# Eight inverse stages taken in pairs, and their banks copied into the product planes

## The chip, the cores and the metric

The kernel runs on one core of one Trainium2 chip. The time is the device time of one execution in microseconds. One execution was also recorded by the hardware profiler; its trace is what the sections below read. PE is the matrix engine, PEld its weight loads, DVE the vector engine, ACT the scalar engine, POOL GpSimd, SP the engine that issues most transfers. PSUM is the memory that PE writes to, eight banks of 128x512 fp32; SBUF is the memory that the other operands lie in.

## The reference

Two branches of one input `x` (2048 x 512), mixed by a gate:

```python
x = A_q
g = _sigmoid((x * gate_w).sum(-1, keepdims=True))
a = _A_ref(x, A_k, A_v, A_shift_k, A_ssm_k, A_ssm_D)
b = _B_ref(x, B_w1, B_w2)          # relu(x @ w1) @ w2, inner width 1792
return g * a + (1 - g) * b
```

The first branch is a long causal convolution over the 2048 positions, for each of 512 channels:

```python
kv = k_shift * v                   # k_shift: 4 taps along the positions
kv_f = rfft(kv padded to 4096)
kf_f = rfft(ssm_k padded to 4096)
y = irfft(kv_f * kf_f)[:2048]
y = y + kv * ssm_D
return q * y
```

## The kernel before

**The MLP branch.** The positions are cut into four chunks of 512, the inner width into 14 tiles. fp32 operands are split into a high and a low part (`xh`, `xl` of x, `hh`, `hl` of the hidden layer, the weights likewise), and each product is three matmuls of 128x512: `mlp1` (L376 to L378) writes a bank `m`; ACT takes `hh` from it (L389), DVE `hl` (L392); `mlp2` (L406 to L408) reads both. The xl parts are made by `split` (L302, `xl_l<-raw,xh_h`), a subtraction that the planner gives to DVE or to POOL. The y sums (L429) take a bank of `mlp2` each. On PE these matmuls are one long stream, and everything else interrupts it.

**The convolution branch.** A transform in two stages. Stage 1 (`s1h`, `s1x`, L459) is over before the place of the change; its result lies in DRAM (`sa`). What follows goes in eight groups g = 0 to 7. For each group a *chain* of PE work, one uninterrupted piece, stands in `conv_mid`: two rounds `f_h` and two rounds `f_x` (L575), 16 small matmuls each on a quarter of the array, into two banks a round. ACT and DVE take `f_h` over into `ha` (L604, L609). Then DVE multiplies (L617): the first product writes `p`, a tile of four planes of 128x512, and four more write `ha`, `qa`, `qb` and `ha` again (called a to e in the code). POOL adds these to `p` in eight sums (L623).

**The inverse.** `inverse(g)` (L642 to L652) reads `p` and the constants `cc` of group g and writes four banks `iv`, with 32 matmuls: one matmul to each bank in turn, eight times. `put_iv` (L654 to L665) empties these banks, DVE the banks 0 and 2 (L664), ACT the banks 1 and 3 (L662), into tiles `bv`, and each tile is stored to DRAM (`sb`, L659). When all is stored, `conv_end` reads it back (`br`) and ends the transform (`cy`, L727).

**Which inverse stands where.** The inverse of group g - 2 (`BEHIND`) stands at the start of the chain of group g; a ninth chain holds the last two inverses, 6 and 7, in a row.

**What sets the order.** The class `Plan` holds all operations with their needs and makes the order of each engine before the program is built, from durations written in the kernel. `room` (L266) says how many buffers of each kind there are: `cv` 8 (PSUM banks), `p` 2 (`PB`), `cc` 3, `bv` 4, `ha` 2, `qa` and `qb` 1. An operation takes and gives back rooms. A PE operation with `pair` waits for a favourable place in the stream, at most the time that `LONG` has for its kind. On each engine the instructions run in the order made; a wait holds up all that stands behind on that engine. The numbers of the banks are dealt out in turn.

Of the kernel before, what the change touches and what calls it, by code (L numbers as in the profile page):

```python
# [13 lines left out]
S, D, DFF = 2048, 512, 1792  # L14
# [3 lines left out]
NJ = 32  # L18
# [216 lines left out]
def act_time(n, psum=False):  # L235
    return n * 0.000833 + (0.05 if psum else 0.093)


def dve_time(n):
    return n * 0.001042 + 0.12  # L240
# [3 lines left out]
TILES = 0.865  # L244
SWITCH = 0.19
ROW = P * D * 4


def build(tc, wf, xp, qn, kn, vn, hn, dn, sh, gw, w1, w2, cs1, ccf, cci, cib, out):
    nc = tc.nc  # L250
# [11 lines left out]
    sb = dram.tile([P, 32, D], F32, name="sb")  # L262

    yd = dram.tile([P, 4, D], F32, name="yd")

    room = {"raw": RAW, "x": 4, "cv": 8, "hh": HB, "o": OB, "in": IN, "cc": BEHIND + 1, "cf": 2, "qa": 1, "qb": 1, "acc": ACC, "tmp": TMP, "ev": EV, "r": RB,  # L266
            "yr": 2, "ha": HAB, "p": PB, "bv": BVB, "br": BRB, "t": TB, "j": 1, "q": QB, "w1": WB, "w2": WB}
    plan = Plan(room)
    add = plan.add
    T = {}  # L270
    cpool = [None, None]

    def tile_of(key, tag, w=D, dt=F32, bufs=None, rows=P, p=None):
        nm = tag + "_" + "_".join(map(str, key[1:] if len(key) > 1 else key))
        T[key] = (p or cpool[0]).tile([rows, w], dt, tag=tag, bufs=bufs or room.get(tag, 1), name=nm)
        return T[key]
# [255 lines left out]


    sbstores = []
    ys, rtags = {}, {}

    def conv_load(g, gate):
        rank = 500.0 + 4 * g
        k = lambda *nm: (*nm, g)
        rtag = lambda t, u: "yr" if (4 * g + 2 * "hx".index(t) + u) % 6 > 3 else "r"  # L540

        def load(t, u):
            tag = rtag(t, u)

            def ld():
                tile_of(k("r", t, u), tag, 2 * D, p=mp if tag == "yr" else None)
                j = 4 * g + 2 * u
                nc.sync.dma_start(rows(T[k("r", t, u)]), sa["hx".index(t), :, j:j + 2])

            return add("SP", ISSUE, rank + 0.1 * u + (0 if t == "h" else 1), ld, [gate], [tag], dma=2 * ROW, fifo=[tag])  # L550

        cc = [add("SP", ISSUE, rank - 0.5, lambda: nc.sync.dma_start(tile_of(k("cf"), "cf", 2 * P), ccf[:, g]), [gate], ["cf"], dma=ROW // 2, fifo=["cf"]),
              add("SP", ISSUE, rank + 1.5, lambda: nc.sync.dma_start(tile_of(k("cc"), "cc", P), cci[:, g]), [gate], ["cc"], dma=ROW // 4, fifo=["cc"])]
        for t in "hx":
            rtags[g, t] = [rtag(t, u) for u in range(2)]
        return [load("h", u) for u in range(2)], [load("x", u) for u in range(2)], cc

    def conv_mid(g, gate):

        rank = (1, 500.0 + 4 * g)  # L560
        k = lambda *nm: (*nm, g)
        tt = nc.vector.tensor_tensor
        chain = []

        def link(dur, fn, deps, take, give=(), pair=0):
            o = add("PE", dur, (0, rank), fn, (deps if not chain else [chain[-1]]), take, give, tiles=True, pair=pair)
            chain.append(o)
            return o

        def rounds(t, o):  # L570
            ps = [bank(k("f", t, o, b)) for b in range(2)]
            for j in range(4):
                for b in range(2):
                    at = slice(64 * b, 64 * b + 64)
                    mm(ps[b][32 * j:32 * j + 32, :], T[k("cf")][at, 64 * j + 32 * o:64 * j + 32 * o + 32],  # L575
                       T[k("r", t, j // 2)][at, (j % 2) * D:(j % 2 + 1) * D], start=True, stop=True)

        old = g - BEHIND
        last = ys.get(old, [])
        if g < NJ // 4:  # L580
            h, x, cc = conv_load(g, gate)
            deps = h + x + cc + last
        else:
            deps = last
        olds = [old] if g < NJ // 4 else range(old, NJ // 4)
        deps = deps + [y for o in olds[1:] for y in ys[o]]
        for o in olds:
            if o >= 0:
                put_iv(o, link(2 * TILES, lambda o=o: inverse(o), deps, ["cv"] * 4, ["p", "cc"], 3 if g == NJ // 4 else 4 if o == olds[0] else 0))
        if g >= NJ // 4:  # L590
            plan.chain(chain)
            return
        planes = lambda z, u, n=2: T[k(z)][:, u * D:(u + n) * D].rearrange("p (r d) -> p r d", d=D)
        ha, fh = [], []
        for o in range(2):
            f = link(TILES, lambda o=o: rounds("h", o), deps, ["cv"] * 2 + ([] if o else ["ha"]), rtags[g, "h"] if o else ())
            fh.append(f)

        plane = lambda i: T[k("ha")][:, i * D:(i + 1) * D]

        def lower(o):
            if not o:
                tile_of(k("ha"), "ha", 4 * D)
            nc.scalar.copy(plane(o), T[k("f", "h", o, 0)])  # L604

        for o in range(2):
            ha.append(add("ACT", act_time(D, True), (0, rank), lambda o=o: lower(o), [fh[o]] + ha[:1], (), ["cv"]))
        for o in (1, 0):
            ha.append(add("DVE", dve_time(D), (0, rank), lambda o=o: tt(plane(2 + o), T[k("f", "h", o, 1)], plane(1 - o), op=OP.add if o else OP.subtract),  # L609
                          [fh[1], ha[1 - o]], (), ["cv"]))  # L610
        fx = [link(TILES, lambda o=o: rounds("x", o), deps, ["cv"] * 2 + ([] if o else ["p"]), [*rtags[g, "x"], "cf"] if o else ()) for o in range(2)]

        def mul(o, b, dst, u, src, n, deps, take=(), give=(), w=None):
            def go():
                if w:
                    tile_of(k(dst), w[0], w[1] * D)
                tt(planes(dst, u, n), T[k("f", "x", o, b)][:, None, :].to_broadcast([P, n, D]), planes("ha", src, n), op=OP.mult)  # L617

            return add("DVE", dve_time(n * D), rank, go, [fx[o], *deps], take, give)

        def sums(dst, src, u, n, deps, sign=1, give=()):
            def go():
                nc.gpsimd.tensor_tensor(planes("p", dst, n), planes("p", dst, n), planes(src, u, n), op=OP.add if sign > 0 else OP.subtract)  # L623

            return add("POOL", 0.11 + n * 1.14, rank, go, deps, (), give)

        a = mul(0, 0, "p", 0, 0, 4, ha, give=["cv"], w=("p", 4))
        b = mul(1, 0, "ha", 2, 2, 2, [a])
        c = mul(1, 0, "qa", 0, 0, 2, [b], ["qa"], ["cv"], ("qa", 2))
        d = mul(0, 1, "qb", 0, 0, 2, [c], ["qb"], ["cv"], ("qb", 2))  # L630
        e = mul(1, 1, "ha", 0, 0, 2, [d], give=["cv"])
        z = sums(3, "ha", 2, 1, [b])
        z = sums(2, "ha", 3, 1, [z], -1)
        z = sums(1, "qa", 0, 1, [z, c])
        z = sums(0, "qa", 1, 1, [z], -1, ["qa"])
        z = sums(2, "qb", 0, 1, [z, d])
        z = sums(3, "qb", 1, 1, [z], 1, ["qb"])
        z = sums(3, "ha", 0, 1, [z, e])
        z = sums(2, "ha", 1, 1, [z], -1, ["ha"])
        ys[g] = [z]  # L640
        plan.chain(chain)

    def inverse(g):
        k = lambda *nm: (*nm, g)
        ps = [bank(k("iv", j)) for j in range(4)]
        for o in range(2):
            for b in range(2):
                for j in range(4):
                    at = slice(32 * j, 32 * j + 32)
                    c = 64 * o  # L650
                    z = (2 * b + o) * D
                    mm(ps[j][64 * b:64 * b + 64, :], T[k("cc")][at, c:c + 64], T[k("p")][at, z:z + D], start=o == 0, stop=o == 1)  # L652

    def put_iv(g, iv):  # L654
        rank = (1, 500.0 + 4 * g)
        k = lambda *nm: (*nm, g)
        for j in range(4):
            def put(j=j):
                nc.sync.dma_start(sb[:, 4 * g + j], T[k("bv", j)])  # L659

            if j % 2:
                bv = add("ACT", act_time(D, True), rank, lambda j=j: nc.scalar.copy(tile_of(k("bv", j), "bv"), T[k("iv", j)]), [iv], ["bv"], ["cv"])  # L662
            else:
                bv = add("DVE", dve_time(D), (0, rank), lambda j=j: nc.vector.tensor_copy(tile_of(k("bv", j), "bv"), T[k("iv", j)]), [iv], ["bv"], ["cv"])  # L664
            sbstores.append(add("SP", ISSUE, (-5000, rank), put, [bv], (), ["bv"], dma=ROW))  # L665


    def finish(n, key, rank, deps, give):
        parts = 2 if n == LAST else 1
# [142 lines left out]

DEBUG = None
SHARE = 0.0
LONG = 50.0, 50.0, 12.0, 0.0
KEEP = 0
SLOW = dict(raw=1.0)
PATIENCE = 0.5
BEHIND = 2
G = 4  # L820
WARM = 9
DMA_AHEAD = 2.0
# [6 lines left out]
ISSUE = 0.47  # L829
IV_FIRST = True  # L830
RAW = 4
WB = 7
HB = 7
TB = 5
OB = 2
# [3 lines left out]
TMP = 1  # L839
RB = 4  # L840
HAB = 2
PB = 2
BVB = 4
BRB = 4
QB = 8
X0 = -31.0
# [44 lines left out]
```

## Time and profile before

| | us |
|---|---|
| median of 3 runs | 385.6 (385.55 to 386.24) |
| the profiled execution | 385.97 |
| its span in the trace | 384.2 |
| PE busy | 379.8 |
| DVE busy | 266.7 |
| ACT busy | 128.8 |
| POOL busy | 91.5 |

The page of the profile gives busy time, the span in 40 slices with the granted clock, the queues, the chain of work that ended last, and the costliest groups. The time outside the span is 1.77 us. A row of the timeline has the start in us from the span's start, the length, the engine, the line, the operation with out<-in, the shape, the number of instructions in the row, and in brackets how long the engine stood idle before it and what ended that. The ends of matmuls are modelled, so the length of a PE stage is read from the start of one stage to the start of the next.

The chains stand in the trace at 183.4 (g = 0), 193.4, 202.7, 219.3, 232.5, 245.7, 258.9, 272.1 (g = 7) and 295.5 (the ninth).

### The profile page before, as it was taken

Reading aid. Unit: us, or ns where it says so; the run is one execution under the profiler, and the core shown is the slowest. Engines: PE = TensorE matmul, PEld = TensorE weight load, DVE = VectorE, ACT = ScalarE, POOL = GpSimd, SP = SyncE. Lnnn points to the kernel's source line nnn. Section 1 sums busy time; section 2 is a strip of 40 time slices with the busy share of each in tenths; the row PEclk is TensorE's granted clock in tenths of the full one; section 3 lists DMA queues with packets and bytes.
Section 4 is the critical chain, followed back from the end, with each engine's and each line's share of the span. In section 5 each row is a group of like instructions: output and inputs, shape, how many; then the busy total and the mean of one; then the engine's idle time right before and its main releaser. Section 6 shows DMA issues by size and latency. Waiting matters only on the chain.

```text
span 384.2 us, 6567 instructions
## 1 busy us (share of the span) xinstructions
PE 379.8 (99%) x2505; PEld 273.8 (71%) x2505; DVE 266.7 (69%) x356; ACT 128.8 (34%) x242; POOL 91.5 (24%) x77
## 2 busy tenths in 40 slices
PE   9999999999999999999999999999999999999996
PEld 5888788668877788788655765565587788688684
DVE  4698999797989028114799687897872347687691
ACT  5643524573147525533224022313400333012100
POOL 0000000000000000000199968866995001000000
PEclk9999999999999999999999999999999999999999
DMA  7997893898648763589867876686460798399331
GB/s 274 368 317 255 298 351 113 293 333 323 208 121 330 295 234 109 185 296 275 285 203 238 307 265 227 241 308 232 139 204 3 241 342 320 120 325 357 117 124 56
DMA packets 43474, 92.51 MB, mean 241 GB/s; under 512 B 4625, under 2 KB 7201, under 8 KB 43442
## 3 DMA queue, kind: packets, MB, share of 16 engines
q1 hardware_dynamic: 43090, 91.77, 68.8%
q8 instruction: 20, 0.33, 0.4%
q10 hardware_dynamic: 288, 0.26, 0.2%
q14 instruction: 12, 0.10, 0.1%
q0 software_dynamic: 64, 0.05, 0.0%
HBM read 61.66 MB, written 30.41 MB: 240 GB/s over the span
## 4 chain that ended last, share of the span: by engine, by line
PE 99%; DVE 0%; DVEq 0%; issue 0%
PE m L406 14%; PE m L407 13%; PE m L408 13%; PE m L376 13%; PE m L377 12%; PE m L378 12%; PE iv L652 4%; PE f_h L575 4%; PE f_x L575 4%; PE m L362 3%; PE s1x L459 2%; PE s1h L459 2%; PE cy L727 2%; PE warm L753 1%; DVE o L677 0%; DVEq L887 0%
## 5 line engine op out<-in xcount | busy, mean ns | idle before, releaser
L623 POOL TENSOR_TENSOR p<-p,ha 128x512 f32<-128x512 f32 x32 | 41.1, 1308 | 202.2 <-DVE ha L617 201.6
L406 PE MATMUL m<-w1h_h,hh 128*128 128x512 f32 x224 | 88.7, 396 | 0.0
L407 PE MATMUL m<-w1l_l,hh 128*128 128x512 f32 x224 | 87.3, 390 | 0.0
L408 PE MATMUL m<-w1h_h,hl 128*128 128x512 f32 x224 | 87.2, 389 | 0.0
L389 ACT ACTIVATE hh<-m 128x512 fp32r<-128x512 f32 x56 | 33.1, 598 | 126.4 <-PE m L378 122.1
L392 DVE SCALAR_TENSOR_TENSOR hl<-m,hh 128x512 fp32r<-128x512 f32 x56 | 38.3, 688 | 44.5 <-ACT hh L389 44.3
L376 PE MATMUL m<-xh_h,w0h_h 128*128 128x512 f32 x160 | 63.0, 394 | 0.0
L377 PE MATMUL m<-xl_l,w0h_h 128*128 128x512 f32 x160 | 62.3, 390 | 0.0
L378 PE MATMUL m<-xh_h,w0l_l 128*128 128x512 f32 x160 | 62.3, 389 | 0.0
L406 PEld LDWEIGHTS m<-w1h_h,hh 128*128 128x128 f32 x224 | 42.0, 188 | 19.1 <-ACT ev L464 6.5
L408 PEld LDWEIGHTS m<-w1h_h,hl 128*128 128x128 f32 x224 | 42.0, 188 | 9.0
L407 PEld LDWEIGHTS m<-w1l_l,hh 128*128 128x128 f32 x224 | 42.1, 188 | 8.3
L376 PEld LDWEIGHTS m<-xh_h,w0h_h 128*128 128x128 f32 x160 | 30.0, 188 | 11.1 <-issue 4.2
L378 PEld LDWEIGHTS m<-xh_h,w0l_l 128*128 128x128 f32 x160 | 30.0, 188 | 6.4
L377 PEld LDWEIGHTS m<-xl_l,w0h_h 128*128 128x128 f32 x160 | 30.0, 188 | 6.0
L518 DVE TENSOR_TENSOR acc<-acc,tmp 128x1024 f32<-128x1024 f32 x24 | 29.3, 1222 | 0.6
L302 DVE TENSOR_TENSOR w1l_l<-raw,w1h_h 128x512 fp32r<-128x512 f32 x14 | 9.4, 686 | 17.7 <-ACT w1h_h L299 17.7
L662 ACT COPY bv<-iv 128x512 f32<-128x512 f32 x16 | 8.7, 589 | 37.1 <-PE iv L652 31.9
L515 DVE TENSOR_TENSOR tmp<-in,sht_sht 128x512 f32<-128x512 f32 x32 | 20.8, 685 | 0.1
L623 POOL TENSOR_TENSOR p<-p,qa 128x512 f32<-128x512 f32 x16 | 20.7, 1317 | 0.0
L617 DVE TENSOR_TENSOR ha<-f_x,ha 128x1024 f32<-128x1024 f32 x16 | 19.5, 1221 | 1.3 <-DVE qb L617 0.5
L623 POOL TENSOR_TENSOR p<-p,qb 128x512 f32<-128x512 f32 x16 | 20.3, 1290 | 0.0
(72 smaller groups left out, 468.1 us busy)
## 6 DMA issues: line engine op xcount, KB each, us to landing
sa<-ev SPq DMA_DIRECT2D x64, 256.0 KB, 3.0
sb<-bv SPq DMA_DIRECT2D x32, 256.0 KB, 3.4
br<-sb SPq DMA_DIRECT2D x16, 512.0 KB, 6.8
raw<-xp SPq DMA_DIRECT2D x28, 256.0 KB, 4.2
raw<-w SPq DMA_DIRECT2D x24, 256.0 KB, 3.8
r_x<-sa SPq DMA_DIRECT2D x12, 512.0 KB, 5.1
in<-kn SPq DMA_DIRECT2D x10, 512.0 KB, 5.0
r_h<-sa SPq DMA_DIRECT2D x10, 512.0 KB, 6.3
```

Source lines behind the costliest of these rows:

```text
L376: mm(ps, part("h", f, k), T["x", "h", xe, c, k], start=k == 0, stop=False)
L377: mm(ps, part("h", f, k), T["x", "l", xe, c, k], start=False, stop=False)
L378: mm(ps, part("l", f, k), T["x", "h", xe, c, k], start=False, stop=k == 3)
L389: nc.scalar.activation(tile_of(("hh", era, c, f), "hh", dt=F32R, p=mp, bufs=HB), T["m1", era, c, f], AF.Relu)
L392: nc.vector.scalar_tensor_tensor(tile_of(("hl", era, c, f), "hl", dt=F32R, p=mp, bufs=HB), T["m1", era, c, f], 0.0, T["hh", era, c, f].bit ...
L406: mm(ps, T["hh", era, c, f][:, z], T["w", "h", 1, f], start=f == fs[0], stop=False)
L407: mm(ps, T["hh", era, c, f][:, z], T["w", "l", 1, f], start=False, stop=False)
L408: mm(ps, T["hl", era, c, f][:, z], T["w", "h", 1, f], start=False, stop=f == fs[-1])
L515: nc.vector.tensor_tensor(o[:, z], T["k", c + (j == 0) + part][:, u], T["sht",][:, j * D:(j + 1) * D], op=OP.mult)
L518: nc.vector.tensor_tensor(T["acc", c], T["acc", c], T[dst], op=OP.add)
L575: mm(ps[b][32 * j:32 * j + 32, :], T[k("cf")][at, 64 * j + 32 * o:64 * j + 32 * o + 32], T[k("r", t, j // 2)][at, (j % 2) * D:(j % 2 + 1) ...
L623: nc.gpsimd.tensor_tensor(planes("p", dst, n), planes("p", dst, n), planes(src, u, n), op=OP.add if sign > 0 else OP.subtract)
```

## The change

- The inverses stand in other chains: the table `INVERSE` says in which. Chain 3 starts with the inverses of groups 0 and 1, chain 5 with 2 and 3, chain 7 with 4 and 5, the ninth with 6 and 7. Chains 2, 4 and 6 have none; these wait for a favourable place up to the 12 us that the fifth number of `LONG` gives.
- The four banks of an inverse are copied back into the tile `p` that it was made from, not into `bv`. The tiles `bv` are gone; the stores read `p`.
- There are three sets of `p` instead of two. A set is taken by the first product on DVE, no longer by the first `f_x` round on PE, and is given back after the fourth store, no longer by the inverse.
- `cc` keeps its three buffers, under a plain number.

```diff
-    room = {"raw": RAW, "x": 4, "cv": 8, "hh": HB, "o": OB, "in": IN, "cc": BEHIND + 1, "cf": 2, "qa": 1, "qb": 1, "acc": ACC, "tmp": TMP, "ev": EV, "r": RB,
-            "yr": 2, "ha": HAB, "p": PB, "bv": BVB, "br": BRB, "t": TB, "j": 1, "q": QB, "w1": WB, "w2": WB}
+    room = {"raw": RAW, "x": 4, "cv": 8, "hh": HB, "o": OB, "in": IN, "cc": 3, "cf": 2, "qa": 1, "qb": 1, "acc": ACC, "tmp": TMP, "ev": EV, "r": RB,
+            "yr": 2, "ha": HAB, "p": PB, "br": BRB, "t": TB, "j": 1, "q": QB, "w1": WB, "w2": WB}
...
-        old = g - BEHIND
-        last = ys.get(old, [])
+        olds = [o for o in range(NJ // 4) if INVERSE[o] == g]
+        deps = [ys[o] for o in range(g - 1) if o in (g - 2, *olds)] + [ys[o] for o in olds if o == g - 1] + [ccs[o] for o in olds]
...
         for o in olds:
-            if o >= 0:
-                put_iv(o, link(2 * TILES, lambda o=o: inverse(o), deps, ["cv"] * 4, ["p", "cc"], 3 if g == NJ // 4 else 4 if o == olds[0] else 0))
+            put_iv(o, link(2 * TILES, lambda o=o: inverse(o), deps, ["cv"] * 4, ["cc"], 3 if g == NJ // 4 else 4 if o == olds[0] else 0))
...
-            f = link(TILES, lambda o=o: rounds("h", o), deps, ["cv"] * 2 + ([] if o else ["ha"]), rtags[g, "h"] if o else ())
+            f = link(TILES, lambda o=o: rounds("h", o), deps, ["cv"] * 2 + ([] if o else ["ha"]), rtags[g, "h"] if o else (), 5 if not chain and g > 1 else 0)
...
-        fx = [link(TILES, lambda o=o: rounds("x", o), deps, ["cv"] * 2 + ([] if o else ["p"]), [*rtags[g, "x"], "cf"] if o else ()) for o in range(2)]
+        fx = [link(TILES, lambda o=o: rounds("x", o), deps, ["cv"] * 2, [*rtags[g, "x"], "cf"] if o else ()) for o in range(2)]
...
-        a = mul(0, 0, "p", 0, 0, 4, ha, give=["cv"], w=("p", 4))
+        a = mul(0, 0, "p", 0, 0, 4, ha, ["p"], ["cv"], ("p", 4))
...
+            def go(j=j):
+                (nc.scalar.copy if j % 2 else nc.vector.tensor_copy)(T["p", g][:, j * D:(j + 1) * D], T["iv", j, g])
+
             def put(j=j):
-                nc.sync.dma_start(sb[:, 4 * g + j], T[k("bv", j)])
+                nc.sync.dma_start(sb[:, 4 * g + j], T["p", g][:, j * D:(j + 1) * D])
...
+            v = add("ACT", act_time(D, True), rank, go, [iv], (), ["cv"]) if j % 2 else add("DVE", dve_time(D), (0, rank), go, [iv], (), ["cv"])
+            sbstores.append(add("SP", ISSUE, (-5000, rank), put, [v], (), ["p"] if j == 3 else (), dma=ROW, fifo=[f"st{g}"]))
...
-LONG = 50.0, 50.0, 12.0, 0.0
+LONG = 50.0, 50.0, 12.0, 0.0, 12.0
-BEHIND = 2
-PB = 2
-BVB = 4
+PB = 3
+INVERSE = 3, 3, 5, 5, 7, 7, 8, 8
```

The planner makes a new order from this. On PE, before the change, the inverse of group 1 at the start of chain 3 (names: `iv_j_g_buffer`, the bank j of group g; `m2_1_3_2` is the MLP tile that it interrupts; in brackets the engines that an instruction waits for):

```order
L408 MATMUL m2_1_3_2_2229<-w1h_h_1_10_1748,hl_1_3_10_1929 128x512
L652 MATMUL iv_0_1_2247<-p_1_2015,cc_1_1913 64x512 [waits DMAHW5_49,DVE_49,Pool_49]
L652 MATMUL iv_1_1_2248<-p_1_2015,cc_1_1913 64x512 [waits DVE_49]
L652 MATMUL iv_2_1_2249<-p_1_2015,cc_1_1913 64x512 [waits DVE_49]
L652 MATMUL iv_3_1_2250<-p_1_2015,cc_1_1913 64x512 [waits DVE_49,PE_49]
L652 MATMUL iv_0_1_2247<-p_1_2015,cc_1_1913 64x512 [waits Pool_49]
```

The same inverse after the change, with the end of the inverse of group 0 ahead of it in the same chain 3:

```order
L649 MATMUL iv_0_0_2204<-p_0_1900,cc_0_1803 64x512
L649 MATMUL iv_1_0_2205<-p_0_1900,cc_0_1803 64x512
L649 MATMUL iv_2_0_2206<-p_0_1900,cc_0_1803 64x512
L649 MATMUL iv_3_0_2207<-p_0_1900,cc_0_1803 64x512
L649 MATMUL iv_0_1_2232<-p_1_2015,cc_1_1914 64x512 [waits DMAHW5_49,DVE_49]
L649 MATMUL iv_1_1_2233<-p_1_2015,cc_1_1914 64x512 [waits DVE_49]
L649 MATMUL iv_2_1_2234<-p_1_2015,cc_1_1914 64x512 [waits DVE_49,PE_49]
L649 MATMUL iv_3_1_2235<-p_1_2015,cc_1_1914 64x512 [waits Activation_49]
```

The inverse of group 1 no longer follows the MLP but another inverse, and its fourth bank waits for ACT.

On DVE, before the change, the stretch of chain 6, from its `ha` to the copy of the next inverse (`hl_1_2_12` and the like belong to the MLP):

```order
L609 TENSOR_TENSOR ha_6_2741<-f_h_1_1_6_2732,ha_6_2741 128x512 [waits PE_49,Activation_49]
L609 TENSOR_TENSOR ha_6_2741<-f_h_0_1_6_2712,ha_6_2741 128x512 [waits Activation_49]
L617 TENSOR_TENSOR p_6_2778<-f_x_0_0_6_2748,ha_6_2741 128x2048 [waits DVE_49,PE_49]
L392 SCALAR_TENSOR_TENSOR hl_1_2_12_2794<-m1_1_2_12_2673,hh_1_2_12_2784 128x512 [waits Activation_49]
L617 TENSOR_TENSOR ha_6_2741<-f_x_1_0_6_2761,ha_6_2741 128x1024 [waits DVE_49,PE_49]
L617 TENSOR_TENSOR qa_6_2808<-f_x_1_0_6_2761,ha_6_2741 128x1024 [waits Pool_49]
L392 SCALAR_TENSOR_TENSOR hl_1_2_13_2821<-m1_1_2_13_2780,hh_1_2_13_2804 128x512 [waits Activation_49]
L617 TENSOR_TENSOR qb_6_2830<-f_x_0_1_6_2749,ha_6_2741 128x1024 [waits Pool_49]
L617 TENSOR_TENSOR ha_6_2741<-f_x_1_1_6_2762,ha_6_2741 128x1024 [waits DVE_49,PE_49]
L302 TENSOR_TENSOR xl_l_1_1_3_2867<-raw_1_1_3_2182,xh_h_1_1_3_2828 128x512 [waits PE_49,Activation_49]
L664 COPY bv_0_5_2882<-iv_0_5_2841 128x512 [waits DMAHW5_49,DMAHW4_49,PE_49]
```

The same stretch after the change, with what now stands ahead of it, up to the copy of the first inverse of chain 7:

```order
L392 SCALAR_TENSOR_TENSOR hl_1_2_13_2723<-m1_1_2_13_2677,hh_1_2_13_2706 128x512 [waits Activation_49]
L302 TENSOR_TENSOR xl_l_1_1_0_2737<-raw_1_1_0_2091,xh_h_1_1_0_2708 128x512 [waits PE_49,Activation_49]
L302 TENSOR_TENSOR xl_l_1_1_1_2743<-raw_1_1_1_2107,xh_h_1_1_1_2721 128x512 [waits PE_49,Activation_49]
L302 TENSOR_TENSOR xl_l_1_1_2_2760<-raw_1_1_2_2123,xh_h_1_1_2_2725 128x512 [waits PE_49,Activation_49]
L302 TENSOR_TENSOR xl_l_1_1_3_2766<-raw_1_1_3_2151,xh_h_1_1_3_2741 128x512 [waits PE_49,Activation_49]
L606 TENSOR_TENSOR ha_6_2745<-f_h_1_1_6_2712,ha_6_2745 128x512 [waits PE_49,Activation_49]
L606 TENSOR_TENSOR ha_6_2745<-f_h_0_1_6_2697,ha_6_2745 128x512 [waits Activation_49]
L614 TENSOR_TENSOR p_6_2784<-f_x_0_0_6_2727,ha_6_2745 128x2048 [waits DMAHW2_49,DMAHW3_49,DMAHW1_49,DMAHW4_49,DVE_49,PE_49]
L614 TENSOR_TENSOR ha_6_2745<-f_x_1_0_6_2747,ha_6_2745 128x1024 [waits DVE_49,PE_49]
L429 TENSOR_TENSOR y8_8_1194<-m2_1_2_0_2762,y8_8_1194 128x512 [waits PE_49]
L614 TENSOR_TENSOR qa_6_2822<-f_x_1_0_6_2747,ha_6_2745 128x1024 [waits Pool_49]
L656 COPY p_4_2451<-iv_0_4_2800 128x512 [waits PE_49]
```

All four xl_l of the next chunk and the last two hl stand ahead of chain 6's `ha`, where before the hl stood among its products and one xl_l behind them, three xl_l being POOL's. The first product of chain 6 also waits for four transfers, the stores of the set of planes it takes, and the copies of the pair stand ahead of the products `qb` and `ha`.

More of the change, by code (lines that the diff above doesn't have):

```diff
@@ L534, in build @@
     sbstores = []
-    ys, rtags = {}, {}
+    ys, rtags, ccs = {}, {}, {}
     def conv_load(g, gate):
@@ L555, in conv_load @@
             rtags[g, t] = [rtag(t, u) for u in range(2)]
+        ccs[g] = cc.pop()
         return [load("h", u) for u in range(2)], [load("x", u) for u in range(2)], cc
@@ L576, in rounds @@
                        T[k("r", t, j // 2)][at, (j % 2) * D:(j % 2 + 1) * D], start=True, stop=True)
-        old = g - BEHIND
-        last = ys.get(old, [])
+        olds = [o for o in range(NJ // 4) if INVERSE[o] == g]
+        deps = [ys[o] for o in range(g - 1) if o in (g - 2, *olds)] + [ys[o] for o in olds if o == g - 1] + [ccs[o] for o in olds]
         if g < NJ // 4:
             h, x, cc = conv_load(g, gate)
[L582 to L586, printed above, removed]
+            deps += h + x + cc
         for o in olds:
-            if o >= 0:
-                put_iv(o, link(2 * TILES, lambda o=o: inverse(o), deps, ["cv"] * 4, ["p", "cc"], 3 if g == NJ // 4 else 4 if o == olds[0] else 0))
+            put_iv(o, link(2 * TILES, lambda o=o: inverse(o), deps, ["cv"] * 4, ["cc"], 3 if g == NJ // 4 else 4 if o == olds[0] else 0))
         if g >= NJ // 4:
@@ L639, in conv_mid @@
         z = sums(2, "ha", 1, 1, [z], -1, ["ha"])
-        ys[g] = [z]
+        ys[g] = z
         plan.chain(chain)
@@ L655, in put_iv @@
         rank = (1, 500.0 + 4 * g)
-        k = lambda *nm: (*nm, g)
         for j in range(4):
+            def go(j=j):
+                (nc.scalar.copy if j % 2 else nc.vector.tensor_copy)(T["p", g][:, j * D:(j + 1) * D], T["iv", j, g])
             def put(j=j):
[L659 to L665, printed above, removed]
+                nc.sync.dma_start(sb[:, 4 * g + j], T["p", g][:, j * D:(j + 1) * D])
+            v = add("ACT", act_time(D, True), rank, go, [iv], (), ["cv"]) if j % 2 else add("DVE", dve_time(D), (0, rank), go, [iv], (), ["cv"])
+            sbstores.append(add("SP", ISSUE, (-5000, rank), put, [v], (), ["p"] if j == 3 else (), dma=ROW, fifo=[f"st{g}"]))
     def finish(n, key, rank, deps, give):
```

## The prediction

> **What bounds the kernel now.** I read the page first: the span, the busy shares, the slices, the granted clock, the chain that ended last, and the group of inverse copies.
>
> ```profile
> span 384.2 us, 6567 instructions
> PE 379.8 (99%) x2505; PEld 273.8 (71%) x2505; DVE 266.7 (69%) x356; ACT 128.8 (34%) x242; POOL 91.5 (24%) x77
> PE   9999999999999999999999999999999999999996
> PEclk9999999999999999999999999999999999999999
> PE 99%; DVE 0%; DVEq 0%; issue 0%
> L662 ACT COPY bv<-iv 128x512 f32<-128x512 f32 x16 | 8.7, 589 | 37.1 <-PE iv L652 31.9
> ```
>
> PE is the chain from start to end, at a full clock. Nothing else is waited for, so only what shortens or stops PE's stream counts. The other engines matter through the eight PSUM banks, which they must empty before PE may write them again.
>
> Next, the timeline around chain 3, the place where a pair will stand.
>
> ```profile
> 219.28 1.97 PE L652 MATMUL iv<-p,cc 32*64 32x512 f32 x32
> 221.19 1.95 PE L575 MATMUL f_h<-r_h,cf 64*32 64x512 f32 x32
> 221.31 1.29 DVE L664 COPY bv<-iv 128x512 f32<-128x512 f32 x2 [3.95 <-PE iv L652]
> 221.40 1.07 ACT L662 COPY bv<-iv 128x512 f32<-128x512 f32 x2 [14.16 <-PE iv L652]
> 222.01 1.83 SPq L659 DMA_DIRECT2D sb<-bv  x4
> 222.04 0.18 PEld L575 LDWEIGHTS f_h<-r_h,cf 64*32 64x32 f32 x15 [0.29 <-ACT bv L662]
> 222.93 1.92 PE L575 MATMUL f_x<-r_x,cf 64*32 64x512 f32 x32
> 224.78 0.50 PE L406 MATMUL m<-w1h_h,hh 128*128 128x512 f32 x1
> ```
>
> Starts tell lengths: inverse to f_h 1.91, f_h to f_x 1.74, f_x to MLP 1.85. Call the start of an inverse T. Its copies begin only when it is over (T+2.03 on DVE, T+2.12 on ACT), and the first ACT copy ends at T+2.71 (221.40 + 0.589). A PE weight load released by that copy begins 0.05 later, at T+2.76. Here this is just in time, because f_h stands between. A second inverse would ask sooner.
>
> **The saving.** The end chain already has two inverses in a row.
>
> ```profile
> 295.48 3.69 PE L652 MATMUL iv<-p,cc 32*64 32x512 f32 x64
> 299.10 0.50 PE L376 MATMUL m<-xh_h,w0h_h 128*128 128x512 f32 x1
> ```
>
> Sixty-four matmuls take 3.62 us: two times 1.73, and one change of shape of 0.16. A single inverse takes 1.91, so a change of shape costs about 0.18. Six inverses with one change each become three pairs: three changes fewer, 3 x 0.18 = **-0.53 us**. The matmuls themselves, and the number of interruptions of the MLP, stay.
>
> **Chains 3 and 5: the fourth bank.** A pair wants eight banks, and one is held by the MLP tile that the chain interrupts. So the eighth request, the fourth bank of the second inverse, gets the bank of the first inverse's first ACT copy (the order rows of chain 3 show that wait on Activation where a PE and DVE wait stood). It is asked for at T+1.73 and free at T+2.76: PE stands for 1.03. PE's queue is in order, so the forward rounds and the MLP behind it stand as well. How much of such a wait is lost, stage 1 shows:
>
> ```profile
> 121.25 1.29 PE L459 MATMUL s1h<-in,s1c_s1t 32*64 32x512 f32 x16
> 128.37 1.06 PE L459 MATMUL s1h<-in,s1c_s1t 32*64 32x512 f32 x16
> ...
> 120.82 0.59 ACT L421 COPY y<-m 128x512 f32<-128x512 f32 x1
> ```
>
> The first of these two s1h stages took 1.29 us, the normal one 1.06. Its last bank was released by the ACT copy that ended at 121.41, 0.16 after its start; 0.05 behind it makes 0.21 of waiting, and the stage was 0.23 longer. So such a wait is lost in full. That gives **+1.0** in chain 3 and, if nothing else is later there, **+1.0** in chain 5. In chain 5 the third bank waits for the last product of chain 4 (in the kernel the banks go round in turn). The rows below put the start of that product at 10.57 after the f_h start (234.38), and its end at 11.79; one hl fewer stands ahead of it in the new order (0.60), so 11.2. In the new order 21 matmuls of the MLP stand between chains 4 and 5; at 0.233 each with the entry (33 of them in the 7.70 from 237.98 to 245.68) they take 4.9, so the second inverse asks 3.59 + 4.9 + 1.73 = 10.2 after that f_h start. That is 1.0 of waiting, beside the 1.03, not added to it.
>
> **Chain 7: the vector engine is late.** The rows for it, from chains 5 and 6 of before:
>
> ```profile
> 234.38 1.95 PE L575 MATMUL f_h<-yr_h,cf 64*32 64x512 f32 x32
> 236.56 1.29 DVE L609 TENSOR_TENSOR ha<-f_h,ha 128x512 f32<-128x512 f32 x2 [0.76 <-PE f_h L575]
> 237.96 2.29 DVE L617 TENSOR_TENSOR p<-f_x,ha 128x2048 f32<-128x2048 f32 x1
> 237.98 0.50 PE L376 MATMUL m<-xh_h,w0h_h 128*128 128x512 f32 x1
> 240.35 1.23 DVE L617 TENSOR_TENSOR ha<-f_x,ha 128x1024 f32<-128x1024 f32 x1
> 241.49 0.68 DVE L392 SCALAR_TENSOR_TENSOR hl<-m,hh 128x512 fp32r<-128x512 f32 x1
> 241.66 2.55 POOL L623 TENSOR_TENSOR p<-p,ha 128x512 f32<-128x512 f32 x2 [3.06 <-DVE ha L617]
> 242.09 1.22 DVE L617 TENSOR_TENSOR qa<-f_x,ha 128x1024 f32<-128x1024 f32 x1
> 243.22 1.22 DVE L617 TENSOR_TENSOR qb<-f_x,ha 128x1024 f32<-128x1024 f32 x1
> 244.95 1.22 DVE L617 TENSOR_TENSOR ha<-f_x,ha 128x1024 f32<-128x1024 f32 x1
> 245.68 1.97 PE L652 MATMUL iv<-p,cc 32*64 32x512 f32 x32
> 245.79 0.60 ACT L389 ACTIVATE hh<-m 128x512 fp32r<-128x512 f32 x1 [2.12 <-PE m L378]
> 246.42 0.69 DVE L392 SCALAR_TENSOR_TENSOR hl<-m,hh 128x512 fp32r<-128x512 f32 x1 [0.25 <-ACT hh L389]
> ```
>
> Call F the start of f_h in chain 6. Before, the ha operations follow at F+2.18. In the new order five DVE instructions stand ahead of them: the hl of the last MLP tile (at F+0.74, as 245.68 to 246.42) and four xl_l, three of which POOL did before. Alone, from F+1.35 at 0.60 each, they put ha at F+3.75. But xl_l and POOL's sums hold each other up:
>
> ```profile
> 206.28 1.36 DVE L302 TENSOR_TENSOR xl_l<-raw,xh_h 128x512 fp32r<-128x512 f32 x1
> ...
> 203.30 3.78 POOL L302 TENSOR_TENSOR xl_l<-raw,xh_h 128x512 fp32r<-128x512 f32 x3
> 207.04 2.99 POOL L623 TENSOR_TENSOR p<-p,qa 128x512 f32<-128x512 f32 x2
> ...
> 249.26 2.54 POOL L623 TENSOR_TENSOR p<-p,ha 128x512 f32<-128x512 f32 x2
> ```
>
> The xl_l took 1.36 us: it stood until POOL ended at 207.08, and the POOL pair behind it took 2.99 instead of 2.54. In the new kernel POOL then runs the sums of chain 5. Eight of them take 10.14 us (241.66 to 251.80 above), from the end of the second product, 7.8 after f_h of chain 5 (7.2 by the rows, and one hl more in between). They end at 17.9 + w, where w is what the first product waits for the stores of its own planes. F stands 15.5 after that f_h: 3.59 for the rounds and 51 x 0.233 for the MLP. So the sums end at F+2.4+w. Those left run between the xl_l; when the last has ended and the four have had their 0.60 each, ha begins, at F+4.8+w.
>
> w: the stores are issued over 1.83 us (row 222.01) and land by the page:
>
> ```profile
> sb<-bv SPq DMA_DIRECT2D x32, 256.0 KB, 3.4
> ```
>
> From T+2.73 + 1.83 + 3.4 the last lands at about T+8.0; the first product would begin 3.58 after f_h (237.96 - 234.38), that is at T + 3.46 + 1.03 + 3.58 = T+8.07. So w is near 0, up to 1.7 with a slow store; I take 0.5, since the median only just fits.
>
> From ha to the copy of the first inverse's bank stand the same operations as from ha to qb before, with a y sum in place of the hl: 6.66 (236.56 to 243.22). The copy and its release take 0.73, so the bank is free at F+4.8+0.5+7.39 = F+12.7. PE wants it, as in chain 5, at F+10.2. The stall is **+2.5**. Bounds: 1.0 (the ACT copy as in chain 3, with xl_l unhindered) and 3.7 (w = 1.7). The second half of f_h then waits for the last product, which ends 3.6 after the copy's start while PE asks 3.3 after it: **+0.3**.
>
> On this lock the Trainium skill, "SBUF — State Buffer", section "SBUF: two separate sides", says that a vector operation with two SBUF inputs and a GpSimd operation take a shared port in turn, each for its whole length. By it the stall is the 2.5 above; if the two only shared, it would be nearer to 1.0. The 1.36 us of the xl_l agrees with the page.
>
> **What costs nothing.** The copies change their target, not shape or number: 0.6 each as above. The products of chains 3 and 5 that wait for stores (w), with everything behind them on DVE, have cover: chain 3's last product ends 11.2 + w after its f_h, and the next chain's f_h comes 3.59 + 48 x 0.233 = 14.8 after it. Beyond w = 3.5 PE would wait, one for one. The eight stores now hold SP for 2 x 1.83 = 3.7 us ahead of the r_x loads; these are wanted one chain later, over 15 us on. Two sets of planes more in flight, three cc and no bv tiles are space. The chains without inverses (2, 4, 6) lose their 1.91 to the pairs and wait for nothing new.
>
> **Sum.** -0.53 + 1.0 + 1.0 + 2.5 + 0.3 = **+4.3**. The profiled execution (385.97, of which 1.77 lies outside the span) becomes 390.2; from the median of the runs shown, 385.6, it is **389.9**. Bounds: +2.5 (chain 7 at its floor), +5.5 (w = 1.7).
>
> **Rivals.**
> - *Faster by the saved changes alone.* Matmuls on other tiles of the array pass the one that waits, and the copy comes early enough. Time 385.6 - 0.5 = 385.1. It decides where the stall of a pair is under 0.18; the copy would have to end 0.85 sooner than the rows put it. Against it is the s1h stage, which lost its wait in full. The Trainium skill, "TensorEngine Tiling (Array Packing)", section "Key Properties", says that changing the mode drains and that tiles execute independently: read so, it gives this 385.1. The 0.18 per change agrees with its first half; the s1h row speaks against carrying the second over a semaphore wait. Chance 0.08.
> - *POOL does not hold DVE in chain 7* (its sums end before the xl_l come): ha at F+3.75, stalls 1.0 to 1.4, no wait at f_h: 388.1 to 388.5. Chance 0.18.
> - *Late stores.* w of 3.5 in chain 5 puts 3.0 more on chain 7: 392.9, and from there chain 3's cover is gone too. For it speaks that eight stores go out one behind the other; the page's 3.4 is against it. Chance 0.07.
> - *It doesn't do what it says*: the waits fall into time that PE lost anyway, and the total stays 385.6. The rows show no such time. Chance 0.05.
>
> **Chances and range.** The forecast (388.5 to 391.2) gets 0.62. With the light case this is 0.80, so the range is 387.8 to 391.2. A measurement of this kernel tells about 0.2%, 0.8 us, from no change. The 385.1 lies just inside; I give 0.03 of its 0.08 to a larger gain. Faster 0.03, same 0.10, slower 0.87.
>
> **What would show it.** Right: the inverse stages of chains 3 and 5 hold a hole of 1.0 before the fourth bank, released by an ACT copy; chain 7's hole is the largest, released by the DVE copy of its own first inverse, with xl_l rows near 1.2 ahead of it; three f_h stages directly after 64 inverse matmuls. Wrong: 64 inverse matmuls in 3.6 us in chains 3, 5 or 7; four xl_l at 0.6 each; a product that stands over 2 us for stores; a hole in chains 2, 4 or 6; or loss in stages before the first chain, which the change doesn't touch.

## The result, and the profile after the change

The changed kernel takes **389.58 us** (median of 4 runs, 389.35 to 390.04), the kernel before 385.81 us in the same session (385.55 to 386.24). The ratio is 1.0098, 95% interval 1.0081 to 1.0115: slower by about 1%. The forecast was 389.9 us, range 387.8 to 391.2. The profiled execution took 389.35 us, with a span of 387.6.

From the page of the changed kernel: the span, the busy times, the slices, the granted clock, the engines of the chain that ended last, and the stores of the inverse banks.

```profile
span 387.6 us, 6575 instructions
PE 383.0 (99%) x2505; PEld 275.4 (71%) x2505; DVE 270.6 (70%) x360; ACT 128.5 (33%) x242; POOL 86.5 (22%) x73
PE   9999999999999999999999999999999999999996
PEclk9999999999999999999999999999999999999999
PE 28%; DVE 2%; DVEq 0%; issue 0%
sb<-p SPq DMA_DIRECT2D x32, 256.0 KB, 3.0
```

The slices and the clock are as before. A hole of 1 us does not show in slices of 9.7 us, least of all when the PE rows have modelled ends. The chain does show something: before, it was PE for 99% of the span; now it adds up to 30%. In order of time it begins here:

```profile
268.62 1.20 DVE ha L606 x2
269.91 2.30 DVE p L614
272.31 1.23 DVE ha L614
273.53 0.59 DVE y L429
274.13 1.14 DVE qa L614
275.41 2.46 PE iv L649 x30
```

PE's inverse in chain 7 waits for DVE, and DVE's row of work is followed back to `ha` of chain 6. There the list of the chain ends; the next rows back on DVE are the four xl_l, and none of them names a wait. So the 30% tells where the list ends, not how much PE bounds: in a run below that still has three holes (e2_xl_pool), the chain is PE for 99% again. The stretch that it points at is the one to read.

The timeline of PE in chain 5 and in chain 7:

```profile
243.66 4.76 PE L649 MATMUL iv<-p,cc 32*64 32x512 f32 x64
248.35 1.99 PE L576 MATMUL f_h<-r_h,cf 64*32 64x512 f32 x32
250.09 1.97 PE L576 MATMUL f_x<-yr_x,cf 64*32 64x512 f32 x32
251.99 0.50 PE L376 MATMUL m<-xh_h,w0h_h 128*128 128x512 f32 x1
...
272.39 5.48 PE L649 MATMUL iv<-p,cc 32*64 32x512 f32 x64
277.80 2.19 PE L576 MATMUL f_h<-yr_h,cf 64*32 64x512 f32 x32
279.54 2.16 PE L576 MATMUL f_x<-r_x,cf 64*32 64x512 f32 x32
281.63 0.50 PE L406 MATMUL m<-w1h_h,hh 128*128 128x512 f32 x1
```

From start to start, chain 5's pair takes 4.69 us and chain 7's 5.41; chain 3's takes 4.60 (215.74 to 220.34). The pair of the ninth chain still takes 3.62. So the holes, the time beyond 3.62, are 0.98, 1.07 and 1.79. The f_x of chain 7 takes 2.09 instead of 1.85 (+0.24), that of chain 5 1.90 (+0.05).

**The sum.** How long the stretch up to the end of stage 1 takes differs from run to run by up to 0.9 us, without regard to the kernel. So I compare from the first MLP matmul after stage 1 to the end of the span, where nothing has yet been changed ahead. These are its rows, of before and of after:

```profile
160.05 0.50 PE L406 MATMUL m<-w1h_h,hh 128*128 128x512 f32 x1
```

```profile
159.73 0.50 PE L406 MATMUL m<-w1h_h,hh 128*128 128x512 f32 x1
```

Before, 384.19 - 160.05 = 224.14; after, 387.57 - 159.73 = 227.84: **+3.70**. The holes, 0.98 + 1.07 + 1.79 + 0.24 + 0.05, make 4.13; the three saved changes of shape, 0.53, come off: 3.60. That leaves 0.10 unplaced. This length of each run is called *the rest* below; it is the sharper measure, the median time the decisive one.

### The profile page after: what moved, and what is told of

Its sections match the earlier page's. It is cut to its first block, busy times and chain, and to the rows that moved or that the text cites. A ratio compares the mean times of both kernels' runs of the same rounds, so it can differ in the third digit from the quotient of the medians.

```text
span 387.6 us, 6575 instructions
## 1 busy us (share of the span) xinstructions
PE 383.0 (99%) x2505; PEld 275.4 (71%) x2505; DVE 270.6 (70%) x360; ACT 128.5 (33%) x242; POOL 86.5 (22%) x73
## 5 line engine op out<-in xcount | busy, mean ns | idle before, releaser
L302 DVE TENSOR_TENSOR xl_l<-raw,xh_h 128x512 fp32r<-128x512 f32 x25 | 19.4, 815 | 2.2 <-ACT xh_h L299 2.2
```

Source lines behind the costliest of these rows:

```text
L302: (nc.gpsimd if eng == "POOL" else nc.vector).tensor_tensor(tile_of(lo, tag + "l", dt=F32R, bufs=bufs, p=p), T[key], T[hi].bitcast(F32), o ...
```

## The experiments

| run | edit to the changed kernel | median us | ratio to before, 95% | rest, us | pair in chain 3, 5, 7, us |
|---|---|---|---|---|---|
| before | | 385.8 | | 224.14 | none |
| the change | | 389.58 | 1.0081 to 1.0115 | 227.84 | 4.60, 4.69, 5.41 |
| e1_single | no pairs | 386.14 | 0.9996 to 1.0014 | 224.20 | none |
| e3_one_pair | pair in chain 5 only | 386.83 | 1.0012 to 1.0030 | 225.18 | -, 4.69, - |
| e2_xl_pool | four xl_l to POOL | 388.83 | 1.0060 to 1.0088 | 227.12 | 4.60, 4.69, 4.60 |
| e8_no_last_sums | two POOL sums left out | 388.99 | 1.0066 to 1.0094 | 227.11 | 4.60, 4.69, 4.66 |
| e4_pair7_at_tile_end | chain 7 held to a tile end, chain 6 early | 387.68 | 1.0035 to 1.0060 | 225.85 | 4.60, 4.69, 3.62 |
| e5_chain6_early | only chain 6 early | 389.29 | 1.0071 to 1.0099 | 227.25 | 4.60, 4.69, 4.69 |
| e6_all_at_tile_end | all pairs held to a tile end | 391.77 | 1.0135 to 1.0163 | 229.94 | 3.62, 3.62, 3.62 |
| e7_single_placed | no pairs, chains 2 and 7 held | 385.88 | 0.9990 to 1.0008 | 224.18 | none |

Each ratio is to the kernel before in the same session, whose median lay between 385.71 and 386.12.

The theory: the loss is the time in which PE stands for a bank inside the pairs, set by the open MLP tile that holds the eighth bank, by the copies, and in chain 7 by late DVE work. The rivals: the loss lies in the other edits (copies into `p`, stores, third set); only DVE's lateness counts and a pair by itself is cheap.

**Pairs alone: e1_single and e3_one_pair.**

```diff
-INVERSE = 3, 3, 5, 5, 7, 7, 8, 8
+INVERSE = 2, 3, 4, 5, 6, 7, 8, 8
```

> One inverse in each of the chains 2 to 7, as before the change (INVERSE = 2, 3, 4, 5, 6, 7, 8, 8); the copies into the product planes, the three sets and the stores from them stay. If the loss is the bank waits of the pairs, all three holes go and three changes of shape come back: 389.6 - 0.98 - 1.07 - 1.79 - 0.24 + 0.53 = 386.0 (385.4 to 386.6). If the loss is in the other edits (products that wait for stores, a third set), it stays at 388.5 or more.

386.14 us, as before the change within the interval. The copies into `p`, their stores and the third set are still in it, so together they cost nothing that can be told from zero; the loss is in the pairs. One edit has no effect in this run, the waiting of chains without an inverse, since no chain lacks one. It was not tested by itself; the stages account for the loss without it, up to the 0.10 us that is unplaced.

```diff
-INVERSE = 3, 3, 5, 5, 7, 7, 8, 8
+INVERSE = 2, 3, 5, 5, 6, 7, 8, 8
```

> One pair only, inverses 2 and 3 in chain 5 (INVERSE = 2, 3, 5, 5, 6, 7, 8, 8); the rest as in the run with single inverses. By the bank waits one pair costs its hole less one change of shape, 1.07 - 0.18 = +0.9 over the run with single inverses, and chain 5's pair takes 4.6 to 4.7. If pairs cost only where DVE is late (chain 7), this run equals the one with single inverses or is 0.2 faster.

386.83, that is 0.7 above the run without pairs by the medians, 0.98 by the rest. One pair with its hole of 1.07 costs this at a place where DVE's last product ends only 0.09 us after the ACT copy (245.55 and 245.46), so the second rival falls.

**Who makes chain 7 worse: e2_xl_pool and e8_no_last_sums.**

```diff
         a = add(first, act_time(D) if first == "ACT" else dve_time(D) / 2, rank, h, [ld], take, fifo=(*take, *(["turn" + first] if turn else [])))
+        if key[:3] == ("x", 1, 1):
+            return a, add("POOL", 1.25, rank, lambda: l("POOL"), [a], (), give)
```

> The changed kernel with the four xl_l ahead of chain 6's products given to POOL instead of DVE. If chain 7 is late because DVE stands in these four (3.51 us with the lock), its products come about 2 us sooner, chain 7's hole falls from 1.79 to 0.8 to 1.1 (the floor set by the copies, as in chains 3 and 5) and the 0.24 before the second f_x goes: 388.6 (388.2 to 389.0). If the hole belongs to the pair itself, whatever DVE did before, it stays at 1.6 or more and the time at 389.5.

The hole in chain 7 is 0.98, and the rest is 0.72 shorter. Here are `ha` of chain 6 on DVE and the pair on PE:

```profile
267.75 1.29 DVE L608 TENSOR_TENSOR ha<-f_h,ha 128x512 f32<-128x512 f32 x2 [1.86 <-ACT ha L603]
...
274.45 4.67 PE L651 MATMUL iv<-p,cc 32*64 32x512 f32 x64
279.05 2.26 PE L578 MATMUL f_h<-yr_h,cf 64*32 64x512 f32 x32
280.79 2.24 PE L578 MATMUL f_x<-r_x,cf 64*32 64x512 f32 x32
282.95 0.50 PE L408 MATMUL m<-w1h_h,hh 128*128 128x512 f32 x1
```

`ha` waits for ACT now, not for DVE's own row of work. What I had expected beside it did not come: f_x still takes 2.16 (+0.31). Here the second half of f_h, and with it all that follows, waits for the first ACT copy of the second inverse: it ends at 280.17, and the weight loads go on at 280.22, 0.30 after they were due (half of the 1.74 from f_h to f_x, at 279.05 + 0.87). So xl_l are not all that can hold this place up. The edit also moved chain 7 in the planner's order, to 9.98 us after f_h of chain 6 (8.62 in the change), so this run alone does not tell what shortened the hole.

The next run keeps the order of every engine and leaves the last two POOL sums of chain 5 out, so that POOL is idle beside the xl_l:

```diff
             def go():
+                if g == 5 and src == "ha" and u < 2:
+                    return
                 nc.gpsimd.tensor_tensor(planes("p", dst, n), planes("p", dst, n), planes(src, u, n), op=OP.add if sign > 0 else OP.subtract)
```

> The changed kernel, its order untouched, with the last two POOL sums of chain 5 left out (the product planes of group 5 lack these terms). POOL is then idle when the four xl_l run on DVE. If POOL's sums hold the xl_l up, the four take 2.4 to 2.6 us instead of 3.51, chain 6's ha begin at F+3.8 instead of F+4.8, and chain 7's hole falls from 1.79 to its floor of 1.0 (the first ACT copy): 388.8 (388.4 to 389.3). If the four are slow by themselves or the number of instructions ahead is what counts, they keep 3.5 us, the hole 1.8 and the time 389.6.

The four xl_l and `ha` on DVE, and the POOL sums beside them, first in the change:

```profile
265.11 3.51 DVE L302 TENSOR_TENSOR xl_l<-raw,xh_h 128x512 fp32r<-128x512 f32 x4
268.55 1.27 DVE L606 TENSOR_TENSOR ha<-f_h,ha 128x512 f32<-128x512 f32 x2
...
263.72 2.55 POOL L620 TENSOR_TENSOR p<-p,ha 128x512 f32<-128x512 f32 x2
```

and without these sums:

```profile
265.67 2.48 DVE L302 TENSOR_TENSOR xl_l<-raw,xh_h 128x512 fp32r<-128x512 f32 x4
268.07 1.28 DVE L606 TENSOR_TENSOR ha<-f_h,ha 128x512 f32<-128x512 f32 x2
```

With the same instructions in the same order, the four take 1.03 less. In the change the first of the four took 1.70 and each of the others 0.68, which is what all four take in e8. POOL's two sums ran until 266.27; from there four times 0.60 reach to 268.67, about where `ha` begin. `ha` begin at F+3.75 (268.07 - 264.32) instead of F+4.78 (268.55 - 263.77). The hole in chain 7 falls to 1.04, and the rest by 0.73. So the part of chain 7's hole above its floor, 0.75 us, comes from the POOL sums that hold DVE up; the four instructions themselves only fill time that the floor covers.

**The open tile: e4_pair7_at_tile_end and e5_chain6_early.** The first holds chain 7 until an MLP tile has ended, and lets chain 6 in without waiting; the second has the latter edit alone.

```diff
-                put_iv(o, link(2 * TILES, lambda o=o: inverse(o), deps, ["cv"] * 4, ["cc"], 3 if g == NJ // 4 else 4 if o == olds[0] else 0))
+                put_iv(o, link(2 * TILES, lambda o=o: inverse(o), deps, ["cv"] * 4, ["cc"], (3 if g in (7, 8) else 4) if o == olds[0] else 0))
...
-            f = link(TILES, lambda o=o: rounds("h", o), deps, ["cv"] * 2 + ([] if o else ["ha"]), rtags[g, "h"] if o else (), 5 if not chain and g > 1 else 0)
+            f = link(TILES, lambda o=o: rounds("h", o), deps, ["cv"] * 2 + ([] if o else ["ha"]), rtags[g, "h"] if o else (), 5 if not chain and g in (2, 4) else 0)
```

> The changed kernel, with chain 7's pair held until an MLP tile has just ended (no open bank) and chain 6 let in without waiting; chains 3 and 5 as in the change. If the eighth bank, held by the open tile, makes the hole, chain 7's pair takes 3.6 like the one in the ninth chain, and chains 3 and 5 keep 4.6: 389.6 - 1.79 - 0.24 = 387.5 (387.0 to 388.0). If the hole is the copies' time whatever tile is open, chain 7 keeps 4.6 or more: 388.8 to 389.6.

> The changed kernel with only the other half of the edit in the run that held chain 7's pair until a tile end: chain 6 is let in without waiting, chain 7's pair starts where it comes, inside an MLP tile. If the open tile makes the hole, chain 7's pair has the floor of 1.0 again and takes 4.6 (not 5.4, since its products are no longer late): 388.6 (388.2 to 389.0). If the earlier chain 6 alone removed the hole, the pair takes 3.6 and the time is that of the run before, 387.7.

The pair of chain 7 on PE, held until the tile end:

```profile
272.29 3.69 PE L649 MATMUL iv<-p,cc 32*64 32x512 f32 x64
275.91 1.95 PE L576 MATMUL f_h<-yr_h,cf 64*32 64x512 f32 x32
```

and with only chain 6 let in early:

```profile
270.03 4.76 PE L649 MATMUL iv<-p,cc 32*64 32x512 f32 x64
274.72 2.27 PE L576 MATMUL f_h<-yr_h,cf 64*32 64x512 f32 x32
276.46 2.25 PE L576 MATMUL f_x<-r_x,cf 64*32 64x512 f32 x32
278.63 0.50 PE L406 MATMUL m<-w1h_h,hh 128*128 128x512 f32 x1
```

At the tile end the pair takes 3.62 and the hole is gone; inside a tile it takes 4.69. The copies are not sooner at the tile end: the first ACT copy begins 2.07 after the pair there (274.36) and 2.07 after it in e5 (272.10), but only in e5 does a weight load of the second inverse have to wait. The last to be waited for in e5 is chain 6's last product, at 272.77, just behind the ACT copy's end at 272.69. The rest falls by 1.99 in the first (1.79 + 0.24 = 2.03 of holes) and by 0.59 in the second. The median of the second, 389.29, is above the 389.0 that was expected at most. f_x still takes 0.32 too long, as in e2; what the rest of the gap is, the runs do not show. (In the profiled execution the stretch ahead of the chains took 0.33 us longer than in that of the change, 160.06 and 159.73, but a median of four runs is not explained by one.)

**All pairs at tile ends: e6_all_at_tile_end.**

```diff
-                put_iv(o, link(2 * TILES, lambda o=o: inverse(o), deps, ["cv"] * 4, ["cc"], 3 if g == NJ // 4 else 4 if o == olds[0] else 0))
+                put_iv(o, link(2 * TILES, lambda o=o: inverse(o), deps, ["cv"] * 4, ["cc"], 3 if o == olds[0] else 0))
```

> The changed kernel with all three pairs held until an MLP tile has just ended. By the open bank every pair takes 3.6 and no hole is left in the chains. If nothing else came of it, 386.1 - 0.5 = 385.6. But each chain waits for a place, the ninth comes 5 to 7 us later than in the change, and with it the last transform, behind which little of the MLP is then left: I expect holes there and 388 to 393.

Every pair takes 3.62, and no hole is left in the chains, as the theory has it; and it is the slowest run of all. The last transform on PE, and the weight loads of it:

```profile
369.75 3.07 PE L723 MATMUL cy<-br,ibt_ibt 64*32 64x512 f32 x48
373.18 1.04 PE L723 MATMUL cy<-br,ibt_ibt 64*32 64x512 f32 x2 [0.36 <-DVE t L733]
374.63 1.09 PE L723 MATMUL cy<-br,ibt_ibt 64*32 64x512 f32 x14 [0.41 <-DVE t L733]
375.65 0.50 PE L406 MATMUL m<-w1h_h,hh 128*128 128x512 f32 x1
```

```profile
373.18 0.13 PEld L723 LDWEIGHTS cy<-br,ibt_ibt 64*32 64x32 f32 x2 [1.27 <-DVE t L733]
374.63 0.18 PEld L723 LDWEIGHTS cy<-br,ibt_ibt 64*32 64x32 f32 x14 [1.31 <-DVE t L733]
```

The chains wait for tile ends, so the ninth starts at 305.6 instead of 298.9 and the last transform at 369.8 instead of 363.0. There it waits for DVE to empty its banks (5.90 instead of 3.59), and after PE's last matmul has begun, 7.9 us pass until the span ends, where the change had 4.0. The transform's 2.3 and the end's 3.8 are more than the 4.1 of holes that are gone; the difference, 2.0, is nearly all of the 2.1 by which the rest is longer than in the change (229.94 and 227.84). What the pairs save comes back at the end, with more on top.

**A placing without pairs: e7_single_placed.**

```diff
-INVERSE = 3, 3, 5, 5, 7, 7, 8, 8
+INVERSE = 2, 3, 4, 5, 6, 7, 8, 8
...
-                put_iv(o, link(2 * TILES, lambda o=o: inverse(o), deps, ["cv"] * 4, ["cc"], 3 if g == NJ // 4 else 4 if o == olds[0] else 0))
+                put_iv(o, link(2 * TILES, lambda o=o: inverse(o), deps, ["cv"] * 4, ["cc"], (3 if g in (2, 7, 8) else 4) if o == olds[0] else 0))
```

> Single inverses as in the run of that name, with the chains 2 and 7 also held until a tile end. No pair but the ninth chain's, so no hole; the bank waits predict the time of the run with single inverses or up to 0.3 less: 385.9 (385.4 to 386.4). If the copies into the product planes had a cost of their own that the earlier run hid, it would show as more than 386.4.

385.88 against 385.89 for before: the same. Again the copies into `p` and their stores cost nothing that can be told from zero. No run here beats the kernel before.

## Why the prediction was right

- **What bounds the kernel**: right. All that PE lost is in stages of PE that wait for a bank, and the profiled executions add up to the difference within 0.10 us.
- **The saving** (-0.53): right in kind. Pairs without a hole take 3.62 us in chains 3, 5 and 7 as in the ninth (e4, e6), where two single inverses take 1.90 each.
- **The fourth bank** (+1.0 each in chains 3 and 5): right, 0.98 and 1.07. The weight loads show who came last; the first row is of chain 3, where the second inverse asks at 215.74 + 1.73, the second of chain 5:

```profile
218.45 0.24 PEld L649 LDWEIGHTS iv<-p,cc 32*64 32x64 f32 x16 [0.79 <-ACT p L656]
...
246.45 0.24 PEld L649 LDWEIGHTS iv<-p,cc 32*64 32x64 f32 x16 [0.89 <-DVE ha L614]
```

  In chain 3 it is the ACT copy, at T+2.71 (forecast T+2.76). In chain 5 the last product of chain 4, which the prediction put level with the copy, came last. That the open tile is what makes it a wait was argued in the prediction; e4 against e5 shows it, and e6 in all three chains.
- **Chain 7** (+2.5): the mechanism was right and the size too large; it measured 1.79. `ha` began at F+4.78 (the sum had F+4.8 + w), and from there to the release of the bank passed 7.36 (7.39):

```profile
275.18 1.28 DVE L656 COPY p<-iv 128x512 f32<-128x512 f32 x2
...
275.91 0.22 PEld L649 LDWEIGHTS iv<-p,cc 32*64 32x64 f32 x14 [0.31 <-DVE p L656]
```

  A bank that qa of chain 6 held came free before that, at 275.38, which is the release that the chain of work above shows; the copy of the first inverse's bank came last. The mis-sized term is **w = 0.5**, the wait of chain 5's first product for the stores. It was 0: the product began 3.58 after its f_h (251.93 - 248.35), as before the change. The stores landed in 3.0 us by the page, not in 3.4. Besides, PE asked at F+10.35 (272.39 + 1.73 - 263.77), not F+10.2. These two, 0.5 and 0.15, are the 0.7 that was too much. One sign came otherwise than named: not every xl_l took near 1.2, but the first 1.70 and three 0.68 each.
- **The last product** (+0.3): right in kind, 0.24 came. The second half of f_h is due 0.87 after its start (277.80 + 0.87 = 278.67), the last product ends at 278.85, and all but the first of these weight loads begin from 278.90 on:

```profile
277.62 1.23 DVE L614 TENSOR_TENSOR ha<-f_x,ha 128x1024 f32<-128x1024 f32 x1
...
278.68 0.39 PEld L576 LDWEIGHTS f_h<-yr_h,cf 64*32 64x32 f32 x15 [0.32 <-issue]
```

  These 0.23 us appear in the f_x stage because f_x's first matmul still starts at its time. In e8 the product ends 1.06 after f_h's start (1.05 in the change), and it is 0.24 again. In e2 and e5 the product ends before f_h starts, and the ACT copy of the second inverse takes its place, with 0.31 and 0.32.
- **What costs nothing**: right by e1 and e7, and by e4: there the first product of chain 7 stood 2.90 us for a store, and the rest fell by the holes all the same. "Two sets of planes more in flight" in that part was a slip: it is one set more.
- **The rivals.** That waiting matmuls are passed by those on other tiles: refuted by three holes of a length that the release times explain. That POOL doesn't hold DVE: refuted by e8. Late stores: in the change none held up chain 3 or 5; chain 7's first product stood 0.51 us for one (it begins 4.20 after f_h, not 3.58), and no stage of PE behind it is longer. That the waits fall into time that PE lost anyway: refuted by the time, and by e1.

The total was 0.3 us above the measured median: 0.7 too much in chain 7, against some smaller gaps the other way (0.10 unplaced, and a median of before 0.2 higher in the later session). That they offset each other is luck; by the stages alone the forecast was 0.7 too high.

## What to carry to other kernels

Putting two stages of one kind back to back saves a change of shape (0.18 us here), but the second stage asks for its banks one stage earlier than the copies can free those of the first; count banks with the accumulator that is open at that place, and compare the copies' end with the moment of the request. Where the pair is moved to a place without an open accumulator, follow what the waiting moves to the end of the kernel, since the hole may come back there. And where instructions of one engine stand ahead of what PE will wait for, look at what a second engine does beside them: the row's length (3.51 us instead of 2.48 for the four xl_l) tells it, though the row names no wait.

## What the runs showed of the hardware

Four vector subtractions with both inputs in SBUF took 3.51 us beside two POOL sums and 2.48 us with POOL idle, in the same order of instructions (the change and e8). That they take turns was expected; the size, about one wait of 1.0 us for the sum under way, all of it in the first subtraction (1.70 us, the others 0.68), is new. Unexpected was the scatter ahead of the chains: the first MLP matmul after stage 1 started between 159.6 and 160.5 us in the ten profiled executions, though the order of work on PE, DVE and ACT is the same up to there, while the rest of the three kernels without pairs agreed within 0.06 us (224.14, 224.20 and 224.18).
